# w_out loaded by two rows with its first rows cast by VectorE, three pairs of first ups, and a seventh buffer of values

## The chip, the core and the metric

The kernel runs on one core of one Trainium2 chip. The metric is device time in microseconds (us). Before the change three runs took 305.78, 306.00 and 306.26 us; their median is 306.0 us.

The core has five instruction streams that matter here: TensorE (PE, with its weight loads shown apart as PEld), VectorE (DVE), ScalarE (ACT), GpSimd (POOL), and SyncE (SP), whose queue issues nearly all DMAs in program order.

## What is computed

A retention layer (attention without a softmax, with a decay per head) followed by a two-layer network with a gated nonlinearity:

```python
# batch, n_heads, seq, head_dim = 8, 8, 576, 64;  d_model 512, d_ff 2048
scores = scale * np.matmul(q, k.transpose(0, 1, 3, 2))
Dmat = np.where(rel >= 0, gamma[:, None, None] ** rel[None, :, :], 0.0)
attn = np.matmul(scores * Dmat[None], v)
x = attn.transpose(0, 2, 1, 3).reshape(B * S, H * D)
h = x @ w_in
g = h * (1.0 / (1.0 + np.exp(-beta * h)))
out = (g @ w_out).astype(np.float32)
```

All inputs and the output are float32 in memory. On the chip the matmuls run in bf16.

## The kernel before, in words

**Retention.** The decay is folded into the operands: q is multiplied by gains `gq` and v by gains `gv`, so what is left of it is a causal mask. A batch has 576 rows; the first 512 are four chunks of 128 (index `c`), and the last 64 rows of two batches together make one of four "tail" chunks (`b` is None). For each chunk the kernel casts k (`kn`, POOL) and multiplies v by its gains (`vn`, POOL, in `pre`), turns q and k so that the head dimension lies on the partitions (PE transposes `t_q`, `t_k` for batches 0 and 1, DMA transposes `x_q`, `x_k`, `x_tail` later), makes masked scores `R` (`a_sc`, L339 and L344), the output of the chunk in PSUM (`a_O`), the part that comes from earlier chunks through a running state (`a_cross`, with the state in `sbd` or `sbq`), and adds k times v to that state (`a_st`, L413 and L416). `a_x` copies the output to `xT`, the left factor of the network. After the last chunk of a batch `a_st` copies the state into `ends`, which only the tails read; for batches 0 and 1 these are four copies of 64 partitions (L427, L428).

**Network.** The rows are worked on in nine blocks of 512. An *up* (`up`, L485; for the first two of block 0 `up_pair`, L500) is four matmuls over the four slices `ko` of d_model into a PSUM buffer `ph`, followed by a Silu on ACT into `gT` (L487, L503); a block has 16 of them (`fo`). A *down* (`down`, L518) multiplies `gT` with rows `fo` of `w_out_sb` and sums 16 of them into `po` for each of four parts `ms` of the block; the result is copied to `ot` and stored. For block 1 the first ten ups are done twice, each on half the columns (256), so that the first half can start when only chunks 0 and 1 of batch 1 are ready.

**Order.** The order of every engine's work is written out by hand (`manual_schedule`). `fill` is the list of ups and downs; `streams` hold everything else with the place in `fill` before which it is put; `merged` weaves them. Block 0's downs start at index `d0` = 16 and block 1's ups at `u1`; `second(6)`, which holds the outputs, `xT` copies and the last state of batch 1, is put at `u1 + 7`.

**Weights.** `w_in` (4 MB) is loaded in eight pieces of 256 columns by SP; pieces 0 and 1 are two DMAs each, by halves of `ko`. DVE casts the odd `ko`, POOL the even ones. `w_out` (4 MB) follows in four loads of four rows `fo` each, into the buffers that w_in's pieces leave (tag "wt", 4 buffers). Each row is multiplied by 1/beta in its cast: in load 0 the odd rows go to POOL, in the others the last row to ACT, and the rest to DVE. Then SP issues q of batch 1, and its k and v.

**PSUM.** Eight banks: three of tag "mm" (`ph`, `po`), two of "O", two of "sc", one for the state.

Of the kernel before, what the change touches and what calls it, by code (L numbers as in the profile page):

```python
# [11 lines left out]
F32 = mybir.dt.float32  # L12
BF16 = mybir.dt.bfloat16
ACT = mybir.ActivationFunctionType
ALU = mybir.AluOpType
# [4 lines left out]
def kernel(  # L20
# [10 lines left out]
    nc = tc.nc  # L31
    B, H, S, D = q.shape
    d_model = H * D
    d_ff = moe_w_in.shape[1]
    N = B * S
    P = 128
    HP = H // 2
    KO = d_model // P
    FO = d_ff // P
    MB = 512  # L40
    CB = MB // P
# [19 lines left out]
    sb = ctx.enter_context(tc.tile_pool(name="sb", bufs=2))  # L61
    psum = ctx.enter_context(tc.psum_pool(name="psum", bufs=1))
# [68 lines left out]
    for h in range(H):  # L131
# [15 lines left out]
                            fill=0.0, base=0, channel_multiplier=-1)  # L147
# [11 lines left out]
    w_out_sb = wpool.tile([P, FO, d_model], BF16, name="w_out_sb")  # L159
    beta_sb = consts.tile([P, FO], F32, name="beta_sb")  # L160
    rbeta_sb = consts.tile([P, FO], F32, name="rbeta_sb")
# [6 lines left out]
    w_out_r = moe_w_out.rearrange("(fo fi) n -> fi fo n", fi=P)  # L168
    wts, whole = {}, [None]

    def load_w_in(g):
        f0, fn = pieces[g]
        if f0 % 512 == 0:
            whole[0] = stage.tile([P, KO, 512], F32, name="wt", tag="wt", bufs=4)
        t = whole[0][:, :, f0 % 512:f0 % 512 + fn]
        for w in (slice(0, 2), slice(2, KO)) if g < 2 else (slice(0, KO),):
            nc.sync.dma_start(t[:, w], w_in_r[:, w, f0:f0 + fn])  # L177
        wts[g] = t

    def cast_w_in(g):  # L180
        t = wts[g]
        f0, fn = pieces[g]
        for ko in range(KO):
            if ko % 2 == 0:
                nc.gpsimd.tensor_copy(w_in_sb[:, ko, f0:f0 + fn], t[:, ko])  # L185
                continue
            nc.vector.tensor_copy(w_in_sb[:, ko, f0:f0 + fn], t[:, ko])

    def load_w_out(g):
        t = stage.tile([P, KO, d_model], F32, name="wt", tag="wt", bufs=4)  # L190
        nc.sync.dma_start(t[:], w_out_r[:, g * KO:(g + 1) * KO, :])
        wts[NP + g] = t

    def cast_w_out(g):
        t = wts.pop(NP + g)
        for i in range(KO):
            fo = g * KO + i
            if i % 2 and g == 0:
                nc.gpsimd.tensor_tensor(w_out_sb[:, fo, :], t[:, i], rbeta_sb[:, fo:fo + 1].to_broadcast([P, d_model]), ALU.mult)  # L199
            elif i == KO - 1:  # L200
                nc.scalar.activation(w_out_sb[:, fo, :], t[:, i], ACT.Copy, scale=rbeta_sb[:, fo:fo + 1])
            else:
                nc.vector.tensor_scalar(w_out_sb[:, fo, :], t[:, i], rbeta_sb[:, fo:fo + 1], None, ALU.mult)  # L203
# [33 lines left out]
    def gains(g, c):  # L237
        return g[:, c, :].unsqueeze(2).to_broadcast([P, H, D])
# [26 lines left out]
    def pre(i, js=(0, 1)):  # L265

        b, c = seq[i]
        if 0 not in js:
            nc.gpsimd.tensor_tensor(live[i]["vn"][:], kv_tiles.pop(i)[:, 1], gains(gv, c), ALU.mult)  # L269
            return  # L270
        vn = sb.tile([P, H, D], BF16, name="vn", tag="vn", bufs=6)
        if b is None:
            t = tail_tiles.pop(c)
            qk = sb.tile([P, 2, H, D], BF16, name="kn", tag="kn", bufs=4)
            qkT = sb.tile([P, 2, HP, P], BF16, name="kT", tag="kT", bufs=4)
            for to, hs in turned:
                nc.gpsimd.tensor_tensor(qk[:, 0, to], t[:, 0, hs], gains(gq, CB)[:, hs], ALU.mult)  # L277
                nc.gpsimd.tensor_copy(qk[:, 1, to], t[:, 1, hs])
            nc.gpsimd.tensor_tensor(vn[:], t[:, 2], gains(gv, CB), ALU.mult)
            live[i] = dict(qk=qk, qkT=qkT, kT=qkT[:, 1], vn=vn)  # L280
            return
        if c % 2 == 0:
            pair[b, c // 2] = (sb.tile([P, 2, H, D], BF16, name="kn", tag="kn", bufs=4),
                               sb.tile([P, 2, HP, P], BF16, name="kT", tag="kT", bufs=4))
        t = kv_tiles[i]
        kn, kT = pair[b, c // 2]
        live[i] = dict(kn=kn[:, c % 2], kT=kT[:, c % 2], vn=vn)
        for to, hs in turned if b >= QB else [(slice(0, H), slice(0, H))]:
            nc.gpsimd.tensor_copy(kn[:, c % 2, to], t[:, 0, hs])  # L289
        if 1 in js:  # L290
            pre(i, (1,))
# [57 lines left out]
    def new_O(i):  # L349
        b, c = seq[i]  # L350
        if split(i):
            tags = ("sc", "sc") if i == CB - 1 else ("O", "sc")
            live[i]["O"] = [psum.tile([P, 2, P], F32, name="O", tag=t, bufs=2) for t in tags]
        else:
            live[i]["O"] = [psum.tile([P, HP, P], F32, name="O", tag="O", bufs=2)]

    def O_of(i, p):
        Os = live[i]["O"]
        return Os[p // 2][:, p % 2] if split(i) else Os[0][:, p]
# [16 lines left out]
    def a_O(i):  # L376

        b, c = seq[i]
        L = live[i]

        early = i < E
        if not early:
            new_O(i)
        R, vn = L["R"], L["vn"]
        crossed = c > 0
        for j, p in [(n % 2, n // 2) for n in range(H)]:
            nc.tensor.matmul(O_of(i, p)[j * D:(j + 1) * D], vn[:, 2 * p + j, :], R[:, j, p, :],  # L387
                             start=opens(i, p) and not (early and crossed), stop=early or not crossed,
                             skip_group_check=True)

    def a_x(i):
        b, c = seq[i]
        x, view = xt(b)[:, :, :, c * PC:(c + 1) * PC], lambda o: o.rearrange("k p (i s) -> k p i s", i=CB)
        Os = live[i]["O"]
        if split(i):
            nc.vector.tensor_copy(x[:, :2], view(Os[0]))
            nc.scalar.copy(x[:, 2:], view(Os[1]))
        else:
            (nc.scalar.copy if i < E + 2 else nc.vector.tensor_copy)(x, view(Os[0]))

    def a_st(i):

        b, c = seq[i]
        if b is None:
            return
        L = live[i]
        if c == 0:
            state_ps[b] = psum.tile([P, HP, P], F32, name="st", tag="st", bufs=1)
        st, tiled = state_ps[b], b >= QB
        for p in range(HP):  # L410
            if tiled:
                for j in range(2):
                    nc.tensor.matmul(st[j * D:(j + 1) * D, p, :D], L["kn"][:, 2 * p + j, :], L["vn"][:, head_of(b, p, j), :],  # L413
                                     start=(c == 0 and p == 0), stop=True, skip_group_check=True)
            else:
                nc.tensor.matmul(st[:, p, :], heads(L["kn"], p), heads(L["vn"], p),  # L416
                                 start=(c == 0 and p == 0), stop=True, skip_group_check=True)
        if tiled:
            nc.scalar.copy((sbq[c] if c < CB - 1 else ends[b])[:], st[:, :, :D])  # L419
            return  # L420
        for j in range(2):
            r, cols = slice(j * D, (j + 1) * D), slice(j * D, (j + 1) * D)
            e = nc.vector.tensor_copy if i == CB + 2 else nc.scalar.copy
            if c < CB - 1:
                e(sbds[c][r, :, cols], st[r, :, cols])
                continue
            e(ends[b][r, :2], st[r, :2, cols])  # L427
            e(ends[b][(1 - j) * D:(2 - j) * D, 2:], st[r, 2:, cols])  # L428
# [60 lines left out]
    phs = {}  # L489

    def up_pair(m, fo, u):

        if m not in gts:
            gts[m] = sb.tile([P, FO, CB, P], BF16, name="gT", tag="gT", bufs=2)
        fs = (fo, fo + 1)
        if u == 0:
            for f in fs:
                phs[f] = psum.tile([P, MB], F32, name="ph", tag="mm", bufs=3)
        for f, ko in [(f, ko) for ko in (0, 1) for f in fs] if u == 0 else [(f, ko) for f in fs for ko in (2, 3)]:
            nc.tensor.matmul(phs[f][:], w_in_sb[:, ko, f * P:(f + 1) * P], xts[m][:, ko],  # L500
                             start=(ko == 0), stop=(ko == KO - 1))
            if ko == KO - 1:
                nc.scalar.activation(gts[m][:, f], phs[f][:], ACT.Silu, scale=beta_sb[:, f:f + 1])  # L503
# [44 lines left out]
    def F(f, *a):  # L548
        return lambda: f(*a)
# [5 lines left out]
    for n in range(4):  # L555
# [33 lines left out]
    warm_up(2, 128)  # L589
    a_cross(3, True)  # L590
    a_O(3)
    a_x(3)
    cast_w_in(0)
    a_st(3)
    cast_w_in(1)
    nc.vector.reciprocal(rbeta_sb[:], beta_sb[:])
# [3 lines left out]
                            fill=0.0, base=0, channel_multiplier=-1)  # L600
    nc.gpsimd.memset(causal2[:TL, TL:], 0.0)

    fill = [F(up_pair, 0, fo, u) for fo in (0,) for u in range(2)] + [F(up, 0, fo) for fo in range(2, FO)]
    d0 = len(fill)
    def down_rows(n):

# [133 lines left out]
```

## Time and profile before

| what | value |
|---|---|
| median of three runs | 306.0 us (305.78 to 306.26) |
| the profiled execution | 306.52 us |
| its span, first to last instruction | 304.8 us |
| granted TensorE clock | 1.000 |
| busy time of PE, ACT, POOL, DVE | 296.8, 134.6, 110.3, 102.6 us |
| bytes moved by DMA | 53.86 MB, 177 GB/s over the span |

The profile is one execution. Its span leaves out what lies before the first and after the last instruction, 1.7 us here. "Busy" adds the durations of an engine's instructions; a matmul's end is modelled, so consecutive matmuls overlap, and it is the distance from start to start that tells how fast they run. In the timeline each row is a run of like instructions: start, time until the end of the last, engine and line, operation, output and inputs, count, and in brackets the engine's idle time before it with what ended it. "<-issue" means that nothing in the profile explains the idle time. The chain that ended last is followed back from the last instruction, at each step to what released it.

### The profile page before, as it was taken

To read this page: it belongs to the slowest core of one execution; us is meant where nothing else is said; L and a number is where in the kernel's file an instruction comes from. 1 tells how busy PE (TensorE), PEld (TensorE's weight loads), DVE (VectorE), ACT (ScalarE), POOL (GpSimd) and SP (SyncE) were. 2 spreads that over 40 slices of the span, in tenths; PEclk is the share of its full clock that TensorE was granted. 3 is DMA by queue.
4 is the path that set the end of the run, shared out by engine and by line. 5 is a ranking of instruction groups with operands and counts; after the bars stand their busy time and mean duration, and the time that the engine had idled before them with its cause. 6 is when DMAs were issued, how large, how long until landed. Compare 5 with 4: busy or idle time off the path is not lost.

```text
span 304.8 us, 5782 instructions
## 1 busy us (share of the span) xinstructions
PE 296.8 (97%) x2345; PEld 151.9 (50%) x2345; DVE 102.6 (34%) x186; ACT 134.6 (44%) x231; POOL 110.3 (36%) x214
## 2 busy tenths in 40 slices
PE   7799999999999999999999999999999999999996
PEld 5554446764544454445444544454454444444444
DVE  5564456504640433133222413151345510020012
ACT  5577546781138313841374127511771057207700
POOL 4666307755753713460418043843452000000000
PEclk9999999999999999999999999999999999999999
DMA  7999999999999799918993899997997110131011
GB/s 200 218 340 363 383 261 245 241 195 241 184 280 242 203 173 241 254 24 158 245 221 70 156 227 251 209 181 184 171 187 137 51 55 0 30 76 34 2 69 69
DMA packets 129210, 53.86 MB, mean 177 GB/s; under 512 B 109968, under 2 KB 122656, under 8 KB 129184
## 3 DMA queue, kind: packets, MB, share of 16 engines
q1 hardware_dynamic: 129152, 53.49, 78.8%
q8 instruction: 18, 0.29, 0.4%
q14 instruction: 8, 0.07, 0.1%
q10 hardware_dynamic: 32, 0.01, 0.0%
HBM read 36.71 MB, written 9.44 MB: 151 GB/s over the span
## 4 chain that ended last, share of the span: by engine, by line
PE 86%; DMA 7%; SPq 5%; POOL 1%; ACT 0%; issue 0%; DVE 0%; POOLq 0%
PE po L518 41%; PE ph L485 36%; SPq L94 3%; DMA wt<-in_moe_w_out_dram 3%; PE sc L339 3%; DMA wt<-in_moe_w_in_dram 2%; PE O L453 2%; PE st L413 2%; DMA kT<-kn 1%; PE O L465 1%; SPq L177 1%; POOL w_out_sb L199 1%; PE O L387 0%; PE st L416 0%; SPq L82 0%
## 5 line engine op out<-in xcount | busy, mean ns | idle before, releaser
L487 ACT ACTIVATE gT<-ph,beta_sb 128x512 bf16<-128x512 f32 (+1 forms) x152 | 99.5, 659 | 81.9 <-PE ph L485 81.5
L518 PE MATMUL po<-w_out_sb,gT 128*128 128x512 bf16 (+2 forms) x608 | 129.7, 368 | 0.3 <-POOL w_out_sb L199 0.3
L485 PE MATMUL ph<-xT,w_in_sb 128*128 128x512 bf16 (+1 forms) x608 | 126.4, 365 | 0.4 <-ACT gT L487 0.4
L485 PEld LDWEIGHTS <-w_in_sb 128*128 128x128 bf16 x608 | 58.4, 98 | 63.0 <-POOL w_in_sb L185 0.8
L518 PEld LDWEIGHTS <-gT 128*128 128x128 bf16 x608 | 56.8, 98 | 64.4 <-issue 1.4
L344 DVE TENSOR_TENSOR R<-sc,causal 128x512 bf16<-128x512 f32 x72 | 45.0, 683 | 81.7 <-PE sc L339 81.6
L525 DVE COPY ot<-po 128x512 f32<-128x512 f32 (+2 forms) x34 | 22.3, 657 | 77.5 <-PE po L518 77.5
L289 POOL CAST kn<-kvn 128x128 bf16<-128x128 f32 (+2 forms) x80 | 25.8, 357 | 56.3 <-DMA kvn<-in_k_dram 55.8
L269 POOL TENSOR_TENSOR vn<-kvn,gv 128x512 bf16<-128x512 f32 x32 | 33.3, 1042 | 12.2 <-DMA kvn<-in_v_dram 5.3
L258 POOL TENSOR_TENSOR qs<-qn,gq 128x256 bf16<-128x256 f32 (+1 forms) x36 | 26.3, 758 | 27.8 <-DMA qn<-in_q_dram 26.5
L419 ACT CAST sbq<-st 128x256 bf16<-128x256 f32 x18 | 6.6, 368 | 35.8 <-PE st L413 35.8
L473 DVE CAST xT<-O 128x512 bf16<-128x512 f32 x20 | 12.7, 685 | 20.2 <-PE O L465 20.2
L339 PE MATMUL sc<-qT,kT 64*128 64x128 bf16 x256 | 10.8, 218 | 0.8 <-ACT kT L320 0.6
L473 ACT CAST xT<-O 128x512 bf16<-128x512 f32 x8 | 4.7, 586 | 13.7 <-PE O L465 13.7
L339 PEld LDWEIGHTS <-kT 64*128 64x128 bf16 x288 | 8.2, 94 | 4.1 <-issue 1.7
L185 POOL CAST w_in_sb<-wt 128x256 bf16<-128x256 f32 x16 | 7.4, 481 | 4.9 <-DMA wt<-in_moe_w_in_dram 4.9
L413 PEld LDWEIGHTS <-kn 128*64 128x64 bf16 x192 | 5.1, 111 | 7.6 <-issue 5.9
L277 POOL TENSOR_TENSOR kn<-tln,gq 128x128 bf16<-128x128 f32 (+1 forms) x12 | 5.6, 470 | 8.0 <-DMA tln<-in_q_dram 5.0
L211 PE MATMUL ph<-warm 128*128 128x128 f32 (+1 forms) x24 | 7.2, 437 | 1.2 <-DVE warm L119 1.2
L453 PE MATMUL O<-R,vn 128*64 128x128 bf16 x224 | 7.7, 220 | 0.0
L203 DVE TENSOR_SCALAR w_out_sb<-wt,rbeta_sb 128x512 bf16<-128x512 f32 x11 | 5.5, 553 | 6.3 <-DMA wt<-in_moe_w_out_dram 6.3
L413 PE MATMUL st<-vn,kn 128*64 128x64 bf16 x192 | 7.4, 200 | 0.0
(70 smaller groups left out, 105.8 us busy)
## 6 DMA issues: line engine op xcount, KB each, us to landing
qn<-in_q_dram SPq DMA_DIRECT2D x16, 512.0 KB, 5.7
kvn<-in_k_dram SPq DMA_DIRECT2D x32, 256.0 KB, 5.1
kvn<-in_v_dram SPq DMA_DIRECT2D x32, 256.0 KB, 5.1
out_dram<-ot SPq DMA_DIRECT2D x31, 256.0 KB, 2.8
wt<-in_moe_w_out_dram SPq DMA_DIRECT2D x4, 1024.0 KB, 10.2
wt<-in_moe_w_in_dram SPq DMA_DIRECT2D x6, 512.0 KB, 8.6
out_dram<-ot SPq DMA_DIRECT2D x9, 128.0 KB, 2.3
wt<-in_moe_w_in_dram SPq DMA_DIRECT2D x4, 256.0 KB, 5.3
```

What stands on the lines that cost most here:

```text
L258: nc.gpsimd.tensor_tensor(batch[b]["qs"][:, cs, to], q_tiles[b][:, hs, cs].rearrange("p h i d -> p i h d"), gq[:, cs, hs].unsqueeze(3).to_ ...
L269: nc.gpsimd.tensor_tensor(live[i]["vn"][:], kv_tiles.pop(i)[:, 1], gains(gv, c), ALU.mult)
L289: nc.gpsimd.tensor_copy(kn[:, c % 2, to], t[:, 0, hs])
L339: nc.tensor.matmul(view(sc[j][:, p, :]), L["kT"][r, p, :], rhs, start=True, stop=True, skip_group_check=True)
L344: nc.vector.tensor_tensor(R[:, j], sc[j][:], m_b, ALU.mult)
L413: nc.tensor.matmul(st[j * D:(j + 1) * D, p, :D], L["kn"][:, 2 * p + j, :], L["vn"][:, head_of(b, p, j), :], start=(c == 0 and p == 0), sto ...
L453: nc.tensor.matmul(out4(i, p, h % 2), L["vn"][:, h, :], rhs if b is None else rhs.rearrange("k (i s) -> k i s", i=CB), start=c % 2 == 0 an ...
L473: (nc.scalar.copy if n == 1 else nc.vector.tensor_copy)(to, O.rearrange("k p i s -> k p (i s)") if b is None else O[:])
L485: nc.tensor.matmul(ph, w_in_sb[:, ko, fo * P:(fo + 1) * P], xts[m][:, ko, :, w], start=(ko == 0), stop=(ko == KO - 1))
L487: nc.scalar.activation(gts[m][:, fo, :, w], ph, ACT.Silu, scale=beta_sb[:, fo:fo + 1])
L518: nc.tensor.matmul(po[:, :nn], gT[:, fo, ms, :], w_out_sb[:, fo, n0:n0 + nn], start=(fo == 0), stop=(fo == FO - 1))
L525: (nc.scalar.copy if m == 0 else nc.vector.tensor_copy)(ot, po[:, :nn])
```

## The change

- `load_w_in`: piece 2 too is loaded by two DMAs.
- `cast_w_in` can take some of the slices `ko`; slices 0 and 1 of piece 0 are cast ahead of `a_x(3)`, slices 2 and 3 behind it.
- `load_w_out`: each load becomes two DMAs of two rows each.
- `cast_w_out`: all four rows of load 0 are cast by DVE. The other loads stay as they were.
- `vn` gets a seventh buffer.
- `a_st`: the copies of the state after the last chunk of batch 1 (`i == CB + 3`) go from ACT to DVE.
- Ups 0 to 5 of block 0 become three pairs. A pair's matmuls go by `ko` and then by up. The pairs take their PSUM buffers from the tags "mm", "O" and "sc" in turn. `d0` stays 16.

```diff
@@ load_w_in
-        for w in (slice(0, 2), slice(2, KO)) if g < 2 else (slice(0, KO),):
+        for w in (slice(0, 2), slice(2, KO)) if g < 3 else (slice(0, KO),):
             nc.sync.dma_start(t[:, w], w_in_r[:, w, f0:f0 + fn])
@@ cast_w_in
-    def cast_w_in(g):
+    def cast_w_in(g, kos=range(KO)):
...
-        for ko in range(KO):
+        for ko in kos:
@@ load_w_out
-        nc.sync.dma_start(t[:], w_out_r[:, g * KO:(g + 1) * KO, :])
+        for w in (slice(0, 2), slice(2, KO)):
+            nc.sync.dma_start(t[:, w], w_out_r[:, g * KO + w.start:g * KO + w.stop, :])
@@ cast_w_out
-            if i % 2 and g == 0:
-                nc.gpsimd.tensor_tensor(w_out_sb[:, fo, :], t[:, i], rbeta_sb[:, fo:fo + 1].to_broadcast([P, d_model]), ALU.mult)
-            elif i == KO - 1:
+            if g and i == KO - 1:
                 nc.scalar.activation(w_out_sb[:, fo, :], t[:, i], ACT.Copy, scale=rbeta_sb[:, fo:fo + 1])
@@ pre
-        vn = sb.tile([P, H, D], BF16, name="vn", tag="vn", bufs=6)
+        vn = sb.tile([P, H, D], BF16, name="vn", tag="vn", bufs=7)
@@ a_st
-            e = nc.vector.tensor_copy if i == CB + 2 else nc.scalar.copy
+            e = nc.vector.tensor_copy if i in (CB + 2, CB + 3) else nc.scalar.copy
@@ up_pair
         if u == 0:
+            tag = ("mm", "O", "sc")[fo // 2]
             for f in fs:
-                phs[f] = psum.tile([P, MB], F32, name="ph", tag="mm", bufs=3)
-        for f, ko in [(f, ko) for ko in (0, 1) for f in fs] if u == 0 else [(f, ko) for f in fs for ko in (2, 3)]:
+                phs[f] = psum.tile([P, MB], F32, name="ph", tag=tag, bufs=3 if tag == "mm" else 2)
+        for ko, f in [(ko, f) for ko in (2 * u, 2 * u + 1) for f in fs]:
@@ order written out
     a_O(3)
+    cast_w_in(0, (0, 1))
     a_x(3)
-    cast_w_in(0)
+    cast_w_in(0, (2, 3))
     a_st(3)
     cast_w_in(1)
...
-    fill = [F(up_pair, 0, fo, u) for fo in (0,) for u in range(2)] + [F(up, 0, fo) for fo in range(2, FO)]
+    fill = [F(up_pair, 0, fo, u) for fo in (0, 2, 4) for u in range(2)] + [F(up, 0, fo) for fo in range(6, FO)]
```

## The prediction

> **What bounds the kernel now.** I read the page's busy times first, then the chain that ended last, then stretches of the timeline wherever the chain leaves TensorE (PE).
>
> ```profile
> PE 296.8 (97%) x2345; PEld 151.9 (50%) x2345; DVE 102.6 (34%) x186; ACT 134.6 (44%) x231; POOL 110.3 (36%) x214
> DMA  7999999999999799918993899997997110131011
> ```
>
> PE is the bound: of 304.8 us it is idle for 8.0, and 4.2 of those lie before 20 us and 3.0 after 250 us, in the last copy and store, which no edit touches. The second line says where else to look: the DMA engines are full from the second slice on, so up to about 63 us a step of PE can be held by the arrival of its data, however early PE is. A 512-column matmul comes every 0.2158 us (64 in 13.81 us, chain, "260.29 13.81"), a 256-column one every 0.108. With these steps I counted when each matmul could have started and looked for what is missing; ends are modelled, so a stall is larger than the idle time shown. Four places lose time: the first downs, the last w_out rows, the change to the second half of block 1's ups, and a tail transpose (0.26 us at 230 us).
>
> ```profile
> 32.09 1.66 DVE L203 TENSOR_SCALAR w_out_sb<-wt,rbeta_sb 128x512 bf16<-128x512 f32 x2 [2.08 <-DMA wt<-in_moe_w_out_dram]
> 32.13 2.51 POOL L199 TENSOR_TENSOR w_out_sb<-wt,rbeta_sb 128x512 bf16<-128x512 f32 x2 [1.87 <-DMA wt<-in_moe_w_out_dram]
> 32.77 0.59 PE L518 MATMUL po<-w_out_sb,gT 128*128 128x512 bf16 x2
> 33.52 1.02 PE L518 MATMUL po<-w_out_sb,gT 128*128 128x512 bf16 x4 [0.16 <-POOL w_out_sb L199]
> 34.70 9.51 PE L518 MATMUL po<-w_out_sb,gT 128*128 128x512 bf16 x42 [0.16 <-POOL w_out_sb L199]
> 40.56 1.28 DVE L203 TENSOR_SCALAR w_out_sb<-wt,rbeta_sb 128x512 bf16<-128x512 f32 x3 [1.86 <-DMA wt<-in_moe_w_out_dram]
> 41.90 1.82 PEld L518 LDWEIGHTS <-gT 128*128 128x128 bf16 x9 [0.30 <-issue]
> 43.64 1.29 DVE L261 TENSOR_TENSOR qs<-qn,gq 128x512 bf16<-128x512 f32 x2 [0.28 <-DMA qn<-in_q_dram]
> 44.72 0.69 POOL L289 CAST kn<-kvn 128x512 bf16<-128x512 f32 x1 [10.07 <-DMA kvn<-in_k_dram]
> 45.36 0.61 PE L313 MATMUL T<-ident,qs 128*128 128x128 bf16 x8
> 45.81 0.39 PE L319 MATMUL T<-ident,kn 128*128 128x128 bf16 x4
> ```
>
> Here (start, duration; idle and releaser in brackets) the reader is to see the two POOL casts of odd rows at 1.25 us each holding PE twice: the third down should start at 33.20 and starts at 33.52, the seventh should follow four steps later, at 34.38, and starts at 34.70. That is 0.32 + 0.32 = 0.64 us. Then fo 14 is the third cast of a load that landed at 40.54, ready at 41.84; its matmul is due at 34.70 + 32 x 0.2158 = 41.61 and starts at 41.90: another 0.29. And the last four rows show what comes next: q and k of batch 1, cast the moment they land.
>
> ```profile
> 57.05 1.29 DVE L399 CAST xT<-O 128x512 bf16<-128x512 f32 x2 [0.64 <-PE O L373]
> 57.30 1.47 PE L485 MATMUL ph<-xT,w_in_sb 128*128 128x256 bf16 x12
> 57.49 0.26 ACT L427 CAST end<-st 64x128 bf16<-64x128 f32 x1 [0.87 <-PE st L416]
> 58.59 3.82 ACT L487 ACTIVATE gT<-ph,beta_sb 128x256 bf16<-128x256 f32 x9
> 59.12 3.11 PE L485 MATMUL ph<-xT,w_in_sb 128*128 128x256 bf16 x27 [0.35 <-ACT gT L487]
> ```
>
> ScalarE (ACT) makes four copies of the last state of batch 1 ahead of its Silus. Three ph buffers fill, and the matmul due at 57.30 + 12 x 0.108 = 58.60 starts at 59.12: 0.52 us.
>
> **The change, part by part.** *First rows of w_out on VectorE (DVE), loads in halves.* Removed: two POOL casts. Added: two DVE casts; alone on the port they come every 0.43 us (three in 1.28). w_out loads land 2.7 us apart, so the first half of load 0 lands about 1.35 us before the whole: estimate 30.65. Rows 0 and 1 are cast by 31.55, rows 2 and 3 between 32.05 and 32.95; the downs want them from 32.7, 33.15, 33.6 and 34.0. The 0.64 goes. PE then reaches load 1 at 32.72 + 12 x 0.2158 = 35.3; its first half is cast by about 34.3, its second by 35.5, wanted at 35.7. Load 3: the last half still lands at 40.54, but fo 14 is now first in its line, ready at 41.1 where PE asks at 40.92; fo 15 (ACT, 0.72) at 41.36 where PE asks at 41.32. So of the 0.29 about 0.22 remains. PE comes to the transposes of q (44.05 now) at 32.72 + 48 x 0.2158 + 0.22 = 43.30, 0.75 early.
>
> *Where that stall goes.* The data are no earlier. q's last quarter is cast at 44.93, its transposes could start at 45.01, PE asks at 44.83: 0.18 of wait. Then k chunk 4 is cast at 45.41 and can be used at 45.48 (0.07 from POOL's end to PE, as at 8.53 and 8.59 us); PE asks at 45.23: 0.25 of wait. The transpose starts at 45.48 in place of 45.81, so **0.33** of the 0.75 is left. Chunk 5 (46.49, asked for at 46.57) takes no more; the v casts have 0.7 us and more to spare.
>
> *Split DMAs.* One more w_in issue and four more w_out issues, all ahead of batch 1's q and k in SP's order. What they add to the stream of loads is the one cost that decides, and the w_in pieces price it:
>
> ```profile
> 19.53 0.29 DVE L187 CAST w_in_sb<-wt 128x256 bf16<-128x256 f32 x1 [0.17 <-DMA wt<-in_moe_w_in_dram]
> 20.29 0.29 DVE L187 CAST w_in_sb<-wt 128x256 bf16<-128x256 f32 x1 [0.46 <-DMA wt<-in_moe_w_in_dram]
> 21.79 0.69 DVE L187 CAST w_in_sb<-wt 128x256 bf16<-128x256 f32 x2 [1.05 <-DMA wt<-in_moe_w_in_dram]
> 23.30 0.70 DVE L187 CAST w_in_sb<-wt 128x256 bf16<-128x256 f32 x2 [0.81 <-DMA wt<-in_moe_w_in_dram]
> ```
>
> Half pieces land 0.76 apart, whole ones 1.50 to 1.51: two halves cost 0.01 to 0.02 more than a whole. Five of them: 0.05 to 0.1. From above: SP takes 0.47 per short issue, 2.35 for five, if nothing covered it. The cover is the backlog: loads issued at 22 to 31 us land 10 us later, and SP is already held by the full queue (2.80 for the second q issue). I take 0, and keep 0.1 as the likely and 2.35 as the far end. The Trainium skill speaks against the edit: "DMA: Bandwidth & Descriptors", Rules for kernel authors, asks for at least 1 MiB per DMA for bandwidth, and its section Anatomy of one DMA fits a fixed 2.0 us to each DMA (for DMAs issued by GpSimd; these are issued by SP). Paid in series, that estimate would put five DMAs at 10 us; the 0.76 against 1.51 contradicts it for a queue that is never empty.
>
> *Casts of w_in ahead of the last x.* DVE is free from 17.6 to 18.34 and the first half piece landed at 16.9, so a 0.35 us cast fits before O is ready; PE starts its first up at 18.91 as before. If the load came after 17.95, x and all of PE would move with it: 0.65 us of cover. *Three pairs:* 24 matmuls in another order, none added; "O" and "sc" banks were last read by 18.82, the pairs come at 20.63 and 22.36. The 64 ups take 13.86 us now against 13.81 worked out, so 0.05 is all there is; it is in the 32.72 above. *Copies of end on DVE:* not seen on DVE in this form. A 128x128 copy takes 0.29 there and a 64x256 cast 0.41; four of 0.29 start after x (58.34) and end by 59.5; behind them DVE has nothing until 70.3. ACT then starts its Silus at about 57.95, frees a buffer by 58.46, and x is ready at 58.42, both before 58.60. **0.52** comes back. *Seventh vn:* POOL's longest wait for one (5.24 us at 202 us) delays casts whose transposes are issued 9 us later in SP's order. I take 0; the bounds are 0 and the 0.26 at 230 us, which follows a queue of SP paced by stores.
>
> After 60 us PE is 0.85 early. The next scores (69.87) need a transpose landed at 67.35, the ones at 75.95 one landed at 73.5: over 2 us to spare. Sum: 0.33 + 0.52 + 0 = **0.85**. The span goes from 304.8 to 303.95. This execution took 306.52 with 1.7 outside its span, the median of the runs is 306.0; taken off the median: **305.15 us**.
>
> **Rivals.** *A, slower: the split loads cost the stream.* Each extra DMA delays q and k by d; PE waits at 45.48 + 5d. From 0.85 / 5 = 0.17 us per DMA the kernel is slower than before. The one row for it: w_out's last load landed 3.1 us after the one before where others took 2.7; 0.43 per DMA gives 5 x 0.43 - 0.85 = +1.3: 307.3. Against: the half pieces of w_in. The Trainium skill's rule from "DMA: Bandwidth & Descriptors" (Anatomy of one DMA) would put d at 2.0 and, as an estimate, the time near 315. *B, only one of the two gains stays.* If loads come 0.3 us later (0.06 per DMA), only 0.52 is left: 305.5; if xT, with 0.18 to spare, takes ACT's place, only 0.33 and a part: 305.6. For it: three slacks under 0.2 us. *C, the loads do not hold PE.* They come 0.4 earlier, or the tail stall falls to the seventh buffer: 0.75 + 0.52, with 0.26 at most 1.5: 304.5 to 304.75. Against: nothing ahead of q in the queue got shorter. *D, nothing moves,* each wait being replaced by its neighbour: 306.0. Against: nothing but ACT holds 58.60.
>
> **How the numbers follow.** Forecast 0.55 (304.9 to 305.4), A 0.07, B 0.21, C 0.12, D 0.05. A measurement of this kernel can tell about 0.2%, 0.61 us, from no change. Forecast and C are faster by more; B and D (0.26) are not, with a little of B's nearer side over the line: faster 0.68, same 0.25, slower 0.07. The range runs from C to nearly D: 304.4 to 306.0.
>
> **What would show it.** No POOL cast of w_out and downs without a gap from 32.7; DVE casts of w_out in twos, the first near 30.7; PE's only waits between 40 and 47 us at the second q transpose and at k chunk 4, the latter at about 45.5; k chunk 4 landing at 44.7 (later would be A or B); the end copies on DVE near 58, and PE without a gap at 58.6. A wait of scores at 69 or 75 us for a transpose, or a different landing of k, would break the sum.

## The result, and the profile after

| | before | after |
|---|---|---|
| median of the runs taken side by side | 306.29 us (305.78 to 307.62) | 304.96 us (304.86 to 306.29) |
| ratio | | 0.9957, 95% interval 0.9945 to 0.9969 |
| the profiled execution, its span | 306.52 us, 304.8 | 305.13 us, 303.4 |

The change makes the kernel 0.3 to 0.55% faster, 1.3 us by the ratio, where 0.85 had been worked out. Busy times and the use of the DMA engines, from the page of after:

```profile
PE 296.7 (98%) x2345; PEld 152.2 (50%) x2345; DVE 104.0 (34%) x192; ACT 133.6 (44%) x227; POOL 108.2 (36%) x212
DMA  8999999999999999909992899997995110131011
```

PE does the same 2345 matmuls in the same busy time, and the span is 1.4 us shorter: so much of its waits is gone. The DMA line reads 9 from the second slice to the thirteenth, which is to about 99 us, before and after (the prediction has 63). Where the waits went is read from the timeline of after, between 30 and 47 us (start, duration, engine and line, operation, count, and in brackets the idle time before with what ended it):

```profile
31.00 0.88 DVE L202 TENSOR_SCALAR w_out_sb<-wt,rbeta_sb 128x512 bf16<-128x512 f32 x2 [0.73 <-DMA wt<-in_moe_w_out_dram]
32.29 0.88 DVE L202 TENSOR_SCALAR w_out_sb<-wt,rbeta_sb 128x512 bf16<-128x512 f32 x2 [0.41 <-DMA wt<-in_moe_w_out_dram]
32.80 10.52 PE L518 MATMUL po<-w_out_sb,gT 128*128 128x512 bf16 x48
33.65 0.88 DVE L202 TENSOR_SCALAR w_out_sb<-wt,rbeta_sb 128x512 bf16<-128x512 f32 x2 [0.47 <-DMA wt<-in_moe_w_out_dram]
36.34 0.88 DVE L202 TENSOR_SCALAR w_out_sb<-wt,rbeta_sb 128x512 bf16<-128x512 f32 x2 [0.86 <-DMA wt<-in_moe_w_out_dram]
39.03 0.88 DVE L202 TENSOR_SCALAR w_out_sb<-wt,rbeta_sb 128x512 bf16<-128x512 f32 x2 [0.85 <-DMA wt<-in_moe_w_out_dram]
40.39 0.49 DVE L202 TENSOR_SCALAR w_out_sb<-wt,rbeta_sb 128x512 bf16<-128x512 f32 x1 [0.48 <-DMA wt<-in_moe_w_out_dram]
43.16 0.61 PE L312 MATMUL T<-ident,qs 128*128 128x128 bf16 x8
44.47 0.72 PE L312 MATMUL T<-ident,qs 128*128 128x128 bf16 x8
44.51 0.70 POOL L288 CAST kn<-kvn 128x512 bf16<-128x512 f32 x1 [13.99 <-DMA kvn<-in_k_dram]
45.27 0.23 PEld L318 LDWEIGHTS <-kn 128*128 128x128 bf16 x4 [0.25 <-POOL kn L288]
45.27 0.40 PE L318 MATMUL T<-ident,kn 128*128 128x128 bf16 x4
```

The 48 downs run as one piece: from 32.80 to the first transposes of q at 43.16 are 10.36 us, which is 48 x 0.2158, with no wait among them. All three stalls of the downs are gone, and 0.89 us with them (the transposes of q, T of q, start at 43.16, 44.05 before). But the transposes of k start only 0.54 earlier, at 45.27 in place of 45.81. The second eight transposes of q take 0.72 us in place of 0.61, a wait of 0.11 for q's last quarter, and ahead of the transposes of k PE waits 0.25 for a cast of k that POOL begins the moment k lands. The chain that ended last passes through the same place:

```profile
34.11 10.35 DMA kvn<-in_k_dram
44.46 0.05 issue
44.51 0.71 POOL kn L288
...
45.27 0.40 PE T L318 x4
```

Up to 44.5 us the end of the kernel now hangs on the load of k, and no longer on PE. The second place is at 57 us, in the timeline of after from 56 us:

```profile
56.52 1.29 DVE L398 CAST xT<-O 128x512 bf16<-128x512 f32 x2 [0.63 <-PE O L372]
56.77 7.57 PE L484 MATMUL ph<-xT,w_in_sb 128*128 128x256 bf16 x60
57.41 5.71 ACT L486 ACTIVATE gT<-ph,beta_sb 128x256 bf16<-128x256 f32 x13 [1.31 <-PE ph L484]
57.73 0.27 DVE L426 CAST end<-st 64x128 bf16<-64x128 f32 x1
58.62 0.29 DVE L427 CAST end<-st 64x128 bf16<-64x128 f32 x1
```

The copies of the state lie on DVE, ACT begins its Silus at 57.41, and the ups go on through 58.07, where the thirteenth is due (56.77 + 12 x 0.108), without a break: 0.52 more. The rest is a wait of the scores of the second tail, which this profile of before has and this one of after has not. It was no part of the forecast. The scores in before, from the timeline of PE:

```profile
229.66 0.98 PE L339 MATMUL sc<-kT 64*128 64x128 bf16 x16
```

and in after:

```profile
228.63 0.66 PE L338 MATMUL sc<-kT 64*128 64x128 bf16 x16
```

The same 16 matmuls take 0.32 us less. So in this pair of executions 0.54 + 0.52 + 0.32 is the 1.4 us of the spans.

### The profile page after: what moved, and what is told of

It reads as the page before. It is cut to its first block, busy times and chain, and to the rows that moved or that the text cites. A ratio compares the mean times of both kernels' runs of the same rounds, so it can differ in the third digit from the quotient of the medians.

```text
span 303.4 us, 5793 instructions
## 1 busy us (share of the span) xinstructions
PE 296.7 (98%) x2345; PEld 152.2 (50%) x2345; DVE 104.0 (34%) x192; ACT 133.6 (44%) x227; POOL 108.2 (36%) x212
## 4 chain that ended last, share of the span: by engine, by line
PE 84%; DMA 8%; SPq 5%; POOL 1%; issue 0%; DVE 0%
PE po L518 38%; PE ph L484 37%; DMA kvn<-in_k_dram 3%; SPq L94 3%; PE sc L338 3%; DMA wt<-in_moe_w_out_dram 3%; PE O L452 2%; DMA wt<-in_moe_w_in_dram 2%; PE st L412 2%; PE O L464 1%; SPq L82 1%; SPq L177 1%; POOL w_in_sb L185 0%; PE O L386 0%; PE T L318 0%
## 5 line engine op out<-in xcount | busy, mean ns | idle before, releaser
L486 ACT ACTIVATE gT<-ph,beta_sb 128x512 bf16<-128x512 f32 (+1 forms) x148 | 97.0, 659 | 82.3 <-PE ph L484 81.9
L484 PE MATMUL ph<-xT,w_in_sb 128*128 128x512 bf16 (+1 forms) x592 | 122.8, 365 | 0.0
L484 PEld LDWEIGHTS <-w_in_sb 128*128 128x128 bf16 x592 | 56.9, 98 | 60.5 <-POOL w_in_sb L185 0.7
L276 POOL TENSOR_TENSOR kn<-tln,gq 128x128 bf16<-128x128 f32 (+1 forms) x12 | 5.7, 471 | 13.9 <-DMA tln<-in_q_dram 7.0
L187 DVE CAST w_in_sb<-wt 128x256 bf16<-128x256 f32 x16 | 5.3, 360 | 6.4 <-DMA wt<-in_moe_w_in_dram 6.4
```

The costliest lines, as they stand in the source:

```text
L484: nc.tensor.matmul(ph, w_in_sb[:, ko, fo * P:(fo + 1) * P], xts[m][:, ko, :, w], start=(ko == 0), stop=(ko == KO - 1))
L486: nc.scalar.activation(gts[m][:, fo, :, w], ph, ACT.Silu, scale=beta_sb[:, fo:fo + 1])
```

## The experiments

Each time is a median with the lowest and highest run; ratios are to the kernel before, run beside it. Its medians were 306.09 us in the first group of kernels (`r_before`, `r_after`, `e_vn6`, `e_endact`), 306.15 in the second (`e_whole`, `e_pool`, `e_oldups`, `e_less`) and 306.31 in the third (`b_enddve`, `b_out`, `e_more`, `e_tail`); so times of different groups are compared only to about 0.2 us. "The cast of k" is that of chunk 4, which begins when it lands; "T(k)" the transposes of it on PE.

**Both kernels once more** (`r_before`, `r_after`), unchanged, for a second pair of profiles.

> The kernel before, unchanged, profiled a second time: what of the differences between the two profiles is chance of one execution. Theory (the halves made the loads earlier): the fourth load of w_out again lands 3.1 us after the third, k chunk 4 of batch 1 near 44.7 us, its transpose at 45.8. Rival (chance): the 3.1 is 2.7 here, k lands near 44.2 to 44.5 with w_in pieces landing as late or early as it happens, and the transpose of k chunk 4 moves by under 0.1 since w_out's casts hold it. The tail scores near 230 us: theory of the seventh buffer, PE waits 0.2 to 0.3 us again; rival (chance in SP's queue), no wait.

> The changed kernel, unchanged, profiled a second time. If the halves speed the loads: k chunk 4 lands 44.4 to 44.5 and its transpose starts at 45.2 to 45.3 again. If that was chance: within 44.2 to 44.8, transpose 45.0 to 45.6, span different by as much. No wait at the tail scores if the seventh buffer took it away.

305.93 and 304.98 us, spans 304.2 and 303.3. The stalls behind POOL's casts and the one at 58 us came again in before and were gone again in after. Two others did not come again: row 14, whose load was earlier (from the seventh down, at 34.71, to T of q at 43.77 are 42 steps and no wait), and the tail:

```profile
229.39 0.67 PE L339 MATMUL sc<-kT 64*128 64x128 bf16 x16
```

This is before with its six buffers of values, second execution: the 16 scores take 0.67 us and wait for nothing. The load of row 14 shows in DVE's casts of the third and fourth load of w_out. The first execution has the third cast at 37.43 and the fourth at 40.56 (the prediction's lines show the latter), 3.13 us apart; the second has them 2.76 apart:

```profile
37.43 1.28 DVE L203 TENSOR_SCALAR w_out_sb<-wt,rbeta_sb 128x512 bf16<-128x512 f32 x3 [1.43 <-DMA wt<-in_moe_w_out_dram]
```

```profile
37.44 1.28 DVE L203 TENSOR_SCALAR w_out_sb<-wt,rbeta_sb 128x512 bf16<-128x512 f32 x3 [1.42 <-DMA wt<-in_moe_w_out_dram]
40.20 1.28 DVE L203 TENSOR_SCALAR w_out_sb<-wt,rbeta_sb 128x512 bf16<-128x512 f32 x3 [1.49 <-DMA wt<-in_moe_w_out_dram]
```

T(k) moved from 45.53 to 45.12, by 0.41, where the first pair has 0.54. In before it came 0.28 earlier than in the first execution (45.81), as T of q did: the wait for row 14 was not there. In after it came 0.15 earlier (45.27), as the cast of k began 0.13 earlier (44.38, and 44.51).

**The seventh buffer taken back** (`e_vn6`).

```diff
-        vn = sb.tile([P, H, D], BF16, name="vn", tag="vn", bufs=7)
+        vn = sb.tile([P, H, D], BF16, name="vn", tag="vn", bufs=6)
```

> The changed kernel with six buffers of values as before. Theory (seventh buffer took the tail stall): PE waits 0.2 to 0.35 us at the scores of the second tail near 229 us, and the time is 0.3 us above the changed kernel: 305.25, ratio to before 0.9967. Rival (the tail stall went by the phase of SP's queue, not by the buffer): no wait, time as the changed kernel, 304.95, ratio 0.9957.

304.95 us (304.84 to 305.46), ratio 0.9968 (0.9955 to 0.998), and no wait at the tail. The buffer is worth nothing that shows; the interval reaches some 0.4 us to either side.

**The end copies back on ACT** (`e_endact`), and, the other way round, **the end copies alone** put into before (`b_enddve`):

```diff
# e_endact, from after
-            e = nc.vector.tensor_copy if i in (CB + 2, CB + 3) else nc.scalar.copy
+            e = nc.vector.tensor_copy if i == CB + 2 else nc.scalar.copy
# b_enddve, from before: the reverse
```

> The changed kernel with the four copies of the last state of batch 1 on ScalarE again. Theory: PE waits 0.5 us for ScalarE near 58 us as before and the time is 0.5 us above the changed kernel: 305.45, ratio to before 0.9973. Rival (the wait is covered now that PE comes earlier or the Silus are ahead): under 0.2 us, ratio 0.996.

> The kernel before with one part of the change alone: the last state of batch 1 copied by VectorE. Theory: PE goes without a gap from the 57.0 us ups into the second halves, 0.5 us are won and nothing else moves: ratio to before 0.9983, about 305.6. Rival (VectorE's later x takes ScalarE's place): under 0.2 us won, ratio above 0.9993.

Without the move 305.65 us (305.28 to 307.18), ratio 0.9991 (0.9977 to 1.0005): 0.70 above `e_vn6` of the same group, 0.44 by the lowest runs. Its timeline has the stall back, with its size:

```profile
57.13 1.47 PE L484 MATMUL ph<-xT,w_in_sb 128*128 128x256 bf16 x12
57.33 0.26 ACT L426 CAST end<-st 64x128 bf16<-64x128 f32 x1 [0.87 <-PE st L415]
58.42 1.63 ACT L486 ACTIVATE gT<-ph,beta_sb 128x256 bf16<-128x256 f32 x4
58.95 1.25 PE L484 MATMUL ph<-xT,w_in_sb 128*128 128x256 bf16 x10 [0.35 <-ACT gT L486]
```

The thirteenth is due at 57.13 + 12 x 0.108 = 58.43 and starts at 58.95: 0.52. Before with the move alone takes 305.50 us (305.32 to 306.68), ratio 0.9979 (0.9971 to 0.9988), which is 0.64 us less (0.37 to 0.89), and its ups pass 58 us without a break.

**w_out's loads whole again** (`e_whole`), all rows of load 0 still cast by DVE.

```diff
-        for w in (slice(0, 2), slice(2, KO)):
-            nc.sync.dma_start(t[:, w], w_out_r[:, g * KO + w.start:g * KO + w.stop, :])
+        nc.sync.dma_start(t[:], w_out_r[:, g * KO:(g + 1) * KO, :])
```

> The changed kernel with each load of w_out in one DMA again (rows of load 0 still all on VectorE). Theory (the arrival of k holds PE at 45 us, so what is lost ahead of it is not felt): row 14 is again cast third, ready 1.3 us after its load lands near 40.2 to 40.5, and PE waits 0.3 to 0.6 us there near 41; its wait for k chunk 4 shrinks by the same, the transpose of k chunk 4 starts within 0.1 of 0.77 us after k lands, and the time is that of the changed kernel, 304.95 to 305.05. Rival (the halves carry the gain): 0.3 to 0.6 us slower than the changed kernel.

305.44 us (305.13 to 305.77), ratio 0.9969 (0.9954 to 0.9984): 0.5 above after and above `e_pool` and `e_oldups` of its own group, and 0.3 by the lowest runs. The timeline:

```profile
32.42 1.67 DVE L201 TENSOR_SCALAR w_out_sb<-wt,rbeta_sb 128x512 bf16<-128x512 f32 x4 [2.08 <-DMA wt<-in_moe_w_out_dram]
32.97 11.16 PE L517 MATMUL po<-w_out_sb,gT 128*128 128x512 bf16 x48
35.07 1.28 DVE L201 TENSOR_SCALAR w_out_sb<-wt,rbeta_sb 128x512 bf16<-128x512 f32 x3 [0.97 <-DMA wt<-in_moe_w_out_dram]
37.77 1.28 DVE L201 TENSOR_SCALAR w_out_sb<-wt,rbeta_sb 128x512 bf16<-128x512 f32 x3 [1.42 <-DMA wt<-in_moe_w_out_dram]
40.48 1.27 DVE L201 TENSOR_SCALAR w_out_sb<-wt,rbeta_sb 128x512 bf16<-128x512 f32 x3 [1.43 <-DMA wt<-in_moe_w_out_dram]
43.96 0.61 PE L311 MATMUL T<-ident,qs 128*128 128x128 bf16 x8
44.60 0.69 POOL L287 CAST kn<-kvn 128x512 bf16<-128x512 f32 x1 [14.01 <-DMA kvn<-in_k_dram]
45.72 0.39 PE L317 MATMUL T<-ident,kn 128*128 128x128 bf16 x4
```

From the first down to T of q are 10.99 us, 0.63 more than 48 steps: each load's first cast cannot begin before all four rows are there. T(k) follows 1.76 behind T of q (twice eight transposes and four downs), as before (44.05 to 45.81), and 1.12 behind the cast of k: PE, and not k, sets it. I had expected k's arrival to cover the loss of the halves. It covers a part: k alone would have let T(k) begin some 0.74 behind its cast (0.76 in after, 0.70 in e_vn6), at 45.34, so 0.38 is lost.

**Rows 1 and 3 back on POOL** (`e_pool`), the loads in halves.

```diff
-            if g and i == KO - 1:
+            if i % 2 and g == 0:
+                nc.gpsimd.tensor_tensor(w_out_sb[:, fo, :], t[:, i], rbeta_sb[:, fo:fo + 1].to_broadcast([P, d_model]), ALU.mult)
+            elif i == KO - 1:
```

> The changed kernel with rows 1 and 3 of w_out cast by GpSimd again, loads still in halves. Theory: row 1 can start at 30.8, half a load earlier, and is ready at 32.1, row 3 at 33.4 to 33.6, wanted at 33.1 and 34.0: no wait of PE from 32.7 to 36, time 304.95 as the changed kernel. So one of the two edits alone does for the first downs. Rival (VectorE is needed): two waits of 0.3 us return at 33.5 and 34.7; the time grows by up to 0.3.

304.97 us (304.84 to 306.01), ratio 0.996 (0.9943 to 0.9978): the same as after. POOL takes 1.3 us for each row still, but starts at 30.78, when the first half has landed:

```profile
30.78 2.62 POOL L200 TENSOR_TENSOR w_out_sb<-wt,rbeta_sb 128x512 bf16<-128x512 f32 x2 [0.53 <-DMA wt<-in_moe_w_out_dram]
32.54 10.52 PE L520 MATMUL po<-w_out_sb,gT 128*128 128x512 bf16 x48
```

The downs run as one piece. It is the halves that carry the gain; the casts on DVE add none that shows once these are there.

**Halves and DVE casts alone** (`b_out`), in before: the two parts of the change in `load_w_out` and `cast_w_out`.

> The kernel before with w_out loaded in halves and all rows of load 0 on VectorE, nothing else. Theory: 0.95 us of waits of PE between 33 and 42 us go, PE then waits for k chunk 4, whose transpose starts 0.7 to 0.8 us after the cast of k begins (1.1 to 1.2 in the kernel before), so 0.35 to 0.45 is left; the wait for ScalarE near 58 us stays 0.5. Ratio 0.9987, about 305.65. Rival (all 0.95 is kept): ratio 0.997.

305.94 us (305.43 to 306.44), ratio 0.9990 (0.9981 to 1.0): 0.31 us less (0 to 0.58). By itself this is hardly clear of no gain, but the interval leaves out the rival's 0.997.

```profile
32.76 10.52 PE L517 MATMUL po<-w_out_sb,gT 128*128 128x512 bf16 x48
44.46 0.68 POOL L288 CAST kn<-kvn 128x512 bf16<-128x512 f32 x1 [14.37 <-DMA kvn<-in_k_dram]
45.20 0.40 PE L318 MATMUL T<-ident,kn 128*128 128x128 bf16 x4
```

The downs run from 32.76 to 43.12, where T of q starts, without a gap, T(k) starts 0.74 behind the cast of k, and the stall at 58 us stays (`0.35 <-ACT gT L486`).

**The first ups as before** (`e_oldups`): piece 2 whole, piece 0 cast behind `a_x(3)`, one pair. (The lines of `up_pair` are put back too; they are not shown.)

```diff
-        for w in (slice(0, 2), slice(2, KO)) if g < 3 else (slice(0, KO),):
+        for w in (slice(0, 2), slice(2, KO)) if g < 2 else (slice(0, KO),):
-    cast_w_in(0, (0, 1))
-    cast_w_in(0, (2, 3))
+    cast_w_in(0)
-    fill = [F(up_pair, 0, fo, u) for fo in (0, 2, 4) for u in range(2)] + [F(up, 0, fo) for fo in range(6, FO)]
+    fill = [F(up_pair, 0, fo, u) for fo in (0,) for u in range(2)] + [F(up, 0, fo) for fo in range(2, FO)]
```

> The changed kernel with the first ups as before: one pair, its matmuls in the old order, casts of w_in all behind the last x, piece 2 in one DMA. Theory: the ups take 13.9 to 14.1 us from first to first down where 13.8 is the least, and the arrival of k covers it: time 304.95 to 305.05. Rival (the pairs matter when w_in comes late): 0.1 to 0.3 us slower.

304.94 us (304.84 to 305.31), ratio 0.9953 (0.9937 to 0.9969): the same as after. The ups took 14.30 us here (18.48 to 32.78) and 14.00 in after (18.80 to 32.80), where 13.9 to 14.1 had been expected here; the first down came at the same time. And with its seven buffers the profiled execution does have a wait at the tail:

```profile
229.14 0.40 PE L338 MATMUL sc<-kT 64*128 64x128 bf16 x8 [0.28 <-DMA kT<-kn]
```

**Less ahead of k** (`e_less`). The second half of w_out's last load is left out (rows 14 and 15 are cast from what rows 12 and 13 left), so 512 KB less lie ahead of q and k.

```diff
-        for w in (slice(0, 2), slice(2, KO)):
+        for w in (slice(0, 2), slice(2, KO))[:1 if g == WG - 1 else 2]:
...
-                nc.vector.tensor_scalar(w_out_sb[:, fo, :], t[:, i], rbeta_sb[:, fo:fo + 1], None, ALU.mult)
+                nc.vector.tensor_scalar(w_out_sb[:, fo, :], t[:, i % 2 if g == WG - 1 else i], rbeta_sb[:, fo:fo + 1], None, ALU.mult)
```

> The changed kernel without the last two rows of w_out's last load: rows 14 and 15 are cast from rows 12 and 13 in their place, 512 KB less ahead of q and k of batch 1. Theory (the stream of loads holds PE at the transposes): q and k land 1.35 us earlier, PE does not wait between 32.7 and 46 us, the transpose of k chunk 4 starts 12.1 us after the first down (12.45 in the changed kernel) and the time is 0.3 us lower, 304.65. Rival (something else holds PE there, the casts or the copies): the transpose stays within 0.1 of 12.45 us and the time stays.

304.73 us (304.44 to 305.42), ratio 0.9944 (0.9926 to 0.9963). Three of its six runs (304.44, 304.47, 304.58) are below every run of after, whose lowest is 304.86. The profiled execution was the slowest of the six:

```profile
34.52 0.49 DVE L202 TENSOR_SCALAR w_out_sb<-wt,rbeta_sb 128x512 bf16<-128x512 f32 x1 [0.46 <-DMA wt<-in_moe_w_out_dram]
36.79 0.88 DVE L202 TENSOR_SCALAR w_out_sb<-wt,rbeta_sb 128x512 bf16<-128x512 f32 x2 [1.79 <-DMA wt<-in_moe_w_out_dram]
38.68 4.92 PE L518 MATMUL po<-w_out_sb,gT 128*128 128x512 bf16 x22 [0.18 <-DVE w_out_sb L202]
43.44 0.61 PE L312 MATMUL T<-ident,qs 128*128 128x128 bf16 x8
43.64 0.70 POOL L288 CAST kn<-kvn 128x512 bf16<-128x512 f32 x1 [13.60 <-DMA kvn<-in_k_dram]
45.20 0.39 PE L318 MATMUL T<-ident,kn 128*128 128x128 bf16 x4
```

Two halves land 2.27 us apart in place of 1.35, and PE waits for a row. T(k) is again 1.76 behind T of q and 1.56 behind the cast of k: with k early, PE sets the time. From the first down to T(k) are 12.48 us, which by the number alone is the rival's sign; but k was not the one waited for, and PE had lost 0.36 to the late half. This execution has the wait at the tail as well: its 16 scores take 1.10 us, 0.44 more than in after. Without the pause T of q would have come at 32.72 + 48 x 0.2158 = 43.08 and T(k) at 44.84, 0.43 ahead of after's; that was not seen in a profile. The lowest run, 0.42 below after's, fits it.

**More ahead of k** (`e_more`). Six buffers, and 384 KB more in three DMAs behind w_out and ahead of q, into places that nobody reads. (The line of `vn` is as in `e_vn6` and not shown.)

```diff
+        if g == WG - 1:
+            more = consts.tile([P, 384], F32, name="more")
+            for to in (more, warm, ident_f):
+                nc.sync.dma_start(to[:], w_out_r[:, g * KO + 3, :to.shape[1]])
```

> The changed kernel, with six buffers of values for the room, and with 384 KB more loaded by three DMAs between w_out and q of batch 1 into places that nobody reads afterwards. Theory (the stream of loads holds PE at 45 us): q and k land 1.0 us later, the transpose of k chunk 4 starts 1.0 us later after the first down, 13.3 to 13.5 us in place of 12.5, and the time is 0.9 to 1.1 us above the changed kernel: 305.95. Rival (PE or a cast holds, loads have slack): under 0.3 us.

306.18 us (306.03 to 307.17), ratio 0.9999 (0.9991 to 1.0008): 1.2 us over after, over `e_vn6` (the same kernel without the loads) and over `e_tail` of its own group.

```profile
32.74 10.52 PE L522 MATMUL po<-w_out_sb,gT 128*128 128x512 bf16 x48
43.45 0.40 PE L316 MATMUL T<-ident,qs 128*128 128x128 bf16 x4 [0.19 <-DVE qs L264]
45.40 0.67 POOL L292 CAST kn<-kvn 128x512 bf16<-128x512 f32 x1 [15.20 <-DMA kvn<-in_k_dram]
46.12 0.40 PE L322 MATMUL T<-ident,kn 128*128 128x128 bf16 x4
```

The downs are untouched; the transposes wait, of q too, and T(k) is 0.72 behind the cast of k. It is 0.85 later than in after, and 1.19 than in the profiled execution of `e_vn6` (44.93), nearly the 1.23 by which the medians differ. For the time 0.9 to 1.1 had been expected.

**The tail's wait attacked directly** (`e_tail`). In SP's order the load of the fourth tail goes behind the transposes of the first two, which are so issued at 218.69 and not at 223.60.

```diff
-                return [(at - 27, F(load_tail, c)), (at - 20, F(load_tail, c + 1)), (at - 17.5, F(pre, i)),
+                return [(at - 27, F(load_tail, c)), (at - 16.4, F(load_tail, c + 1)), (at - 17.5, F(pre, i)),
```

> The changed kernel with the load of the fourth tail put behind the transposes of the first two in SP's order. Theory (the wait of PE at the second tail's scores is a race with SP's queue): these transposes are issued near 218.5 us in place of 223.7, land 4 us before PE needs them, the wait is gone in every execution, and the median falls by 0.05 to 0.15 to 304.85 with a narrower spread. Rival (the fourth tail's own transpose, 2.7 us later, becomes the wait at 236 us): the same or up to 0.5 us slower.

304.98 us (304.93 to 305.22), ratio 0.996 (0.9948 to 0.9972), no wait in the profiled execution. The time is that of after, so this gave nothing that the runs can tell, and no version here that does all the work is clearly faster than after.

## Why the prediction was right, and where it was off

The forecast was 305.15 us, and 304.96 was measured. Both gains of its sum are there for the reasons given: each lowers the time when put into before alone (`b_enddve`, and `b_out` at the edge of the noise), and taking back the end copies or the halves costs time (`e_endact`, `e_whole`). That leaves no room for rivals B and D.

**The downs, 0.33: right.** The bound that the prediction set on this gain, k's arrival, is what the runs show. The kernels fall into two kinds. Where loads are whole (before twice, the end copies alone, e_whole), T(k) starts 1.09, 1.19, 1.11 and 1.12 behind the cast of k, always 1.75 or 1.76 behind T of q: PE sets it. In nearly all with halves it starts 0.69 to 0.84 behind the cast, and k sets it; e_less is the exception that was built to be one. The two means (1.13 and 0.74) are 0.39 apart, near the 0.33 forecast, and before with this part alone gained 0.31 (0 to 0.58). The first pair of profiles has 0.54, of which 0.21 is k itself: its cast began at 44.51, where the sum went by the 44.72 of before. The two waits of the sum are there in after with their sizes: 0.11 at q's last quarter (0.18 forecast) and 0.25 at k (0.25). Three details of the step:

- Row 14 was to keep 0.22 of its 0.29; it kept nothing, since the cast of the last half began at 40.39, where the sum had it land at 40.54, and PE came 0.08 later. In the second execution of before even the 0.29 was missing. It didn't matter: k took what this gave, as the 0.25 of idle time ahead of T(k) shows.
- The step took halves and DVE casts together. Alone, the casts are worth less than the halves (e_whole), and with the halves nothing that shows (e_pool).
- In e_vn6, where k landed at 44.23, T(k) was 1.79 behind T of q: k and PE were then nearly equally late. What k leaves of the gain changes by some tenths from one execution to the next.

**Split DMAs, 0: right, and rival A refuted.** In after, the halves of w_out from the second on land 1.34 to 1.36 us apart, and two of them make 2.69 (33.65, 36.34, 39.03); whole loads in e_whole make 2.70 and 2.71. SP comes to its first k load behind them at 34.11, and in before at 34.09. Five more DMAs cost nothing that shows here. On this the Trainium skill, "DMA: Bandwidth & Descriptors", Rules for kernel authors, asks for at least 1 MiB per DMA for the highest bandwidth. For these loads it does not hold: halves of 512 KB lose no time while the queue behind them is never empty.

**End copies, 0.52: right.** 0.52 is what the profile of e_endact has back, and by times it is 0.64 (0.37 to 0.89) in before. Each copy takes 0.27 to 0.29 on DVE, as estimated from a larger one.

**Pairs and early casts, 0; seventh buffer, 0: right.** Neither shows in a time when taken back. In after the early cast had less room than the prediction gave it: DVE began it at 17.50, and POOL waited for the same half piece until 17.53, where the prediction has it landed at 16.9 and sets the limit at 17.95.

**What was off: the tail, and the base.** The prediction called the tail's wait "a queue of SP paced by stores" and kept it at its 0.26. With six buffers, before and b_out have it, and r_before, e_vn6, b_enddve and e_more have none; with seven, e_endact, e_whole, e_oldups and e_less have it, and after, r_after, e_pool and e_tail have none. So it is a wait of 0.2 to 0.45 us, by the time that the 16 scores take, that one execution has and the next has not, whatever the buffers. The one profile of before happened to have it, and a late last load of w_out too.

The step that was off is the last one, "taken off the median", 306.0 of three runs, and with it the size of the gain. Beside after, the median of before was 306.29, so the base was 0.29 too low; the gain was 1.33 and not 0.85, so the sum was 0.48 too small. The two errors have opposite signs, and that 305.15 lies only 0.19 from 304.96 is in part luck. The lowest runs of before in the groups were 305.76 to 305.87, that of after was 304.86 (304.84 in `e_vn6`, `e_pool` and `e_oldups`), so the lowest differ by 0.9 to 1.0, near the 0.85 forecast; the two parts put into before one at a time lower it from 305.87 in that group by 0.55 (305.32) and 0.44 (305.43).

The other 0.3 to 0.4 of the medians' difference is spread: before's median lies 0.3 to 0.5 above its lowest run, that of after 0.1. A part of before's spread can be named. Its two profiled executions differ by 0.59 (306.52 and 305.93), and the two waits that only the slower one has, 0.32 at the tail and 0.28 for row 14, make 0.60. But after and its variants meet such waits too, and how often each kernel does, fourteen profiles cannot tell. Median less lowest run is 0.37 and 0.51 in the kernels with the end copies on ACT (e_endact, b_out), 0.18 in b_enddve, 0.31 in e_whole, 0.29 in e_less, and 0.05 to 0.15 in the other variants of after. Why the end copies, or PE's slack against k, should widen the spread was not tried and stays open.

Rival C, by which the loads do not hold PE, is refuted in its cause: 384 KB more cost 1.2 us, and 512 KB less gave 0.2 by medians and 0.4 by the lowest runs. So a further gain at 45 us has to begin with fewer bytes ahead of k, or with an earlier place for k, which was not tried; behind the first 0.4 or so PE itself is the next limit (`e_less`).

## What to carry to other kernels

Before a gain is summed, look for the next arrival of data behind it: 0.9 us of stalls went away here, and k's load let 0.4 to 0.5 through. Split a load when its consumers begin with its first rows and the queue is never empty, and measure that alone before moving casts between engines. A stall of 0.3 us that one profile shows may be that execution's own; take a second profile before giving it a cause or a place in the sum.

## What the runs showed of the hardware that was not expected

The stream of loads pauses. In six of the fourteen profiled executions one load or half of w_out lands 0.3 to 0.9 us later than its place in the steady step (1.35 us for a half, 2.70 for a whole load): 0.4 in before, 0.6 in e_endact, 0.9 in e_less, 0.33 in b_out, and about 0.3 in e_tail and b_enddve. r_before, the same kernel as before, has none. It follows no edit, and its cause is open. Where it falls, k lands later: its cast began at 44.72 in before and at 44.34 in r_before.

A cast on DVE can be held for most of a cast on POOL. In before, DVE's first cast of w_out takes 0.49 us and its second, beside POOL's first (1.33), 1.26; in after two take 0.88. In e_pool, where each of DVE's first two casts began just ahead of one of POOL's, DVE's take 0.49 and POOL's 1.32 and 1.34: so in before it was DVE that waited, and POOL was no slower than there. This agrees with the Trainium skill, "SBUF — State Buffer", Who interferes with whom, by which the two engines share a pair of ports that one of them holds for a whole instruction.
